# Block 0 of a two-layer kernel: V of the first two tiles from raw x, mended afterwards with weight column sums and norm rows

## The chip, the cores and the metric

The kernel runs on one core of a Trainium2 chip. A core has five engines that run side by side: TensorE (PE, matmuls), VectorE (DVE), ScalarE (ACT), GpSimd (POOL) and SyncE (SP, which here only issues DMAs). The metric is the device time of one execution in microseconds (us); less is better. The time before is 1616.42 us, the median of three runs (1616.15 to 1616.79).

## The reference

The input is one sequence of 2048 tokens with 1024 channels, in bfloat16. Two kinds of layer follow each other twice:

```python
x = x + _A_ref(_layernorm(x), wqkv, wo)                  # attention
x = x + _B_ref(_layernorm(x), W_gate, W_up, W_down)      # gated feed-forward
x = x + _A_ref(_layernorm(x), wqkv, wo)
x = x + _B_ref(_layernorm(x), W_gate, W_up, W_down)
```

`_A_ref` projects the normalized x to Q, K and V, with 32 heads of 32 channels. Each token attends to eight earlier tokens, at distances 0, 2, ..., 14; the softmax runs over these eight, and the result is projected by `wo`. `_B_ref` computes a gate and an up projection of width 3584, multiplies the up projection by the gate's positive part, and projects down. Layer normalization subtracts the mean over the 1024 channels and multiplies by 1/sqrt(variance + 1e-5); call that factor rstd.

## The kernel before

**Tiles and blocks.** The tokens are cut into 16 tiles of 128 (`P`), four tiles (`TPB`) to a block of 512 (`BLK`). All x stays in SBUF, one tile per 128 tokens, in bf16. A projection needs the normalized x with channels on the partitions (`xnT`); it is turned either by PE (a transpose into PSUM and a copy out of it) or by a DMA transpose on SP (`turn`, L282). The 1024 channels are eight chunks of 128 (`kc`), so one output tile of 128 channels by 512 tokens (a "c step") is eight matmuls of 512 columns.

**Weights.** They come in slabs of 1 MB on SP's DMA queue into a ring of five (`wring`); the load of a slab waits on SP until the slab five before it has been read for the last time. The two slabs of V for block 0 are special (`load_slab`, L226): each is loaded in four slices of one chunk, so that the first matmul need not wait for a whole slab. Slabs `v0,0` and `v0,1` hold the chunks 0 to 3 and 4 to 7. Q's two halves, K's two halves and later slabs follow on the same queue, with the x tiles of the next blocks between them.

**Order of the work.** PE instructions are chained in the order in which the program emits them (`pe_group`), those of DVE in the first pass by `dv`, and the DMAs on SP by `sp_dma`; each queue runs strictly in order. The emission order comes from a list of events with planned times (L957 to L1129): `t_v0`, `t_qk0` and so on are starting times of the stages, `GRP` (1.73) is the planned time of one c step. The planned times only sort the events.

**Stages of the first pass.** V of block 0 (`v_first`, L482), Q and K of block 0 (L1014), Q and K of block 1 (staged to DRAM), V of blocks 1 and 2, then within them the head sums of block 0 (`head_mm`, L640) for the softmax of block 0, V of block 3, Q and part of K of blocks 2 and 3, the output projection of block 0 (`wo_steps`, L808), the rest of K, and then the gate and up projections of block 0. DVE meanwhile forms the products of Q with shifted K for block 0 (`prod_sum_steps`, L654), whose sum is the tile `s`; PE adds the heads of `s` (tile `L`); DVE and ACT make the softmax; DVE multiplies by V (`pv_steps`), starts the Q-K products of block 1, and adds the output projection to x (`add`, L828). These additions stand on DVE behind the first products of block 1. The accumulators of all projections share one PSUM ring of six (`psum`, L81), a second area of two banks (`psum_l`) holds `L` and some transposes.

**V of block 0 (L512 to L557).** Nine scratch matmuls run while x is loaded (L442). Tile 0 is centred first: DVE and ACT each sum half of the channels and DVE subtracts the mean (`centre`). PE transposes the centred tile, ACT copies it to `xnT`, and matmuls on single chunks of tile 0 begin. Tile 1 is centred with the batch-norm statistics of DVE (`bn`, `aggr`), turned in two halves between matmuls of tile 0, and joined. The rstd of both tiles is applied afterwards: POOL computes it, splits it into three bf16 parts (`thirds`), PE spreads it over the partitions (`spread_rstd`, tile `rb`), and DVE multiplies V with it on the way out of PSUM (`scaled`) and later `xnT` for Q and K (`widen`). Tiles 2 and 3 are normalized in full before they are turned; their turns and copies (`later`) stand between matmuls of other tiles.

The emission order around the head sums of block 0 is

```python
    spread(v_steps(2, ln_a[2], "v123", True), t_v2, GRP)
    ev.append((t_v2 + 5.2 * GRP, lambda: head_mm(0)))
    spread(softmax_steps(0), t_v2 + 5.3 * GRP, 0.01)
```

so the head sums stand behind the sixth c step of V of block 2.

Of the kernel before, what the change touches and what calls it, by code (L numbers as in the profile page):

```python
# [7 lines left out]
BF16 = mybir.dt.bfloat16  # L8
# [28 lines left out]
def kernel(  # L37
# [123 lines left out]
    k_d = dram.tile([KC, P, S], BF16, name="k_d")  # L161
    s_d = [dram.tile([P, TPB, W, P], BF16, name=f"s_d{i}") for i in range(2)]
# [8 lines left out]
    def load_x(b, tiles=range(TPB)):  # L171
        for t in (b * TPB + i for i in tiles):
            if t == 0:
                sp_dma(x_tiles[t][:, 0:SLAB], x_dram[t * P:(t + 1) * P, 0:SLAB])
                nc.scalar.dma_start(x_tiles[t][:, SLAB:D], x_dram[t * P:(t + 1) * P, SLAB:D])
            elif t == 1:
                nc.scalar.dma_start(x_tiles[t][:], x_dram[t * P:(t + 1) * P, :])
            else:
                sp_dma(x_tiles[t][:], x_dram[t * P:(t + 1) * P, :])
# [42 lines left out]
    def load_slab(key, src):  # L222
# [3 lines left out]
        if key[0] == "v0":  # L226
            for i, (k0, k1) in enumerate(((0, 1), (1, 2), (2, 3), (3, 4)) if key[1] == 0 else ((0, 1), (1, 2), (2, 3), (3, 4))):
                if (key[1], i) == (1, 2):
                    load_x(0, [2, 3])
                sp_dma(tv[:, k0:k1, :], src[:, k0:k1, :])  # L230
# [76 lines left out]
    load_slab(("qk01", "q", 0), qkv_half(0, 0))  # L307
# [10 lines left out]
    def ln_first():  # L318
        hold = {"xnT": xnT_pool.tile([P, TPB, KC, P], BF16, tag="xnT", name="xnT_first")}
        xna = big_tile([P, TPB, D], "xn_first", True)  # L320
        last = {}
# [20 lines left out]
        def aggr(t):  # L342
# [3 lines left out]
            power(t, mv[:, 1:2], 1.0)  # L346

        pair = stat_pool.tile([P, 2], F32, tag="rpair", name="rpair", bufs=1)

        def power(t, var, sign):  # L350
            vpe = small("vpe1")
            rstd[t] = pair[:, t:t + 1] if t < 2 else small("rstd1")[:]
            on("g", nc.gpsimd.tensor_scalar, vpe[:], var, sign, EPS, op0=ALU.mult, op1=ALU.add)
            on("g", nc.gpsimd.tensor_tensor, rstd[t], vpe[:], neg_half[:, 0:1], op=ALU.pow)

        def centre():
            parts = [small("part0"), small("part1")]
            on("v", nc.vector.tensor_scalar, xna[:, 0, 0:SLAB], x_tiles[0][:, 0:SLAB], 1.0 / D, None, op0=ALU.mult,
               op1=ALU.add, accum_out=parts[0][:])
            on("a", nc.scalar.activation, xna[:, 0, SLAB:D], x_tiles[0][:, SLAB:D], ACT.Identity, scale=1.0 / D,  # L360
               accum_out=parts[1][:])
            for h in range(2):
                cols = slice(h * SLAB, (h + 1) * SLAB)
                on("v", nc.vector.tensor_scalar, xna[:, 0, cols], x_tiles[0][:, cols], parts[0][:], parts[1][:],
                   op0=ALU.subtract, op1=ALU.subtract)

        def centre_second():
            for h in range(2):
                cols = slice(h * SLAB, (h + 1) * SLAB)
                on("v", nc.vector.tensor_scalar, xna[:, 1, cols], x_tiles[1][:, cols], mean[1], None, op0=ALU.subtract)  # L370

        def square_of(src):
            sq = small("sq1")
            on("a", nc.scalar.activation, xna[:, 3, :], src, ACT.Square, scale=float(D) ** -0.5, accum_out=sq[:])
            return sq

        def act_mean(t):
            mn = small("mean1")
            on("a", nc.scalar.activation, xna[:, t, :], x_tiles[t][:], ACT.Identity, scale=1.0 / D, accum_out=mn[:])
            mean[t] = mn[:]  # L380

        def act_power(t, sq):
            nvar = small("nvar1")
# [778 lines left out]
```

## Time and profile before

| | |
|---|---|
| median of three runs | 1616.42 us |
| span of the profiled execution, first to last instruction | 1614.4 us |
| median over that span (what lies around it) | 2.0 us |
| PE busy | 1607.8 us (100%) |
| DVE busy | 1141.5 us (71%) |
| ACT busy | 474.9 us (29%) |
| DMA moved | 317.94 MB, mean 197 GB/s |
| granted PE clock, mean | 1.000 |
| Q of block 0 starts on PE | 22.00 us |
| output projection of block 0 starts on PE | 157.33 us |

The page does not give a time of its own for the profiled execution beside its span; the three runs agree within 0.64 us. The profile is a record of one execution. "Busy" of PE counts pipelined matmuls, so it says that PE always has one in flight and not that each goes at its best pace. The chain of waits is followed back from the last instruction: each piece is what the next one had to wait for. In a timeline, the columns are start and duration in us, engine, line, operation, output and inputs, and in brackets the idle time of that engine just before and what ended it.

### The profile page before, as it was taken

The numbers are of one execution on the slowest core, as the hardware profiler recorded it, in microseconds if no ns is written. First come the engines' busy times: TensorE is split into PE (matmuls) and PEld (weight loads), VectorE is DVE, ScalarE is ACT, GpSimd is POOL, SyncE is SP. The second block draws the span as 40 slices with busy tenths as digits, with TensorE's granted clock in tenths as the row PEclk, the third lists the DMA queues.
The fourth block names the chain that finished last, engine by engine and source line by source line (L and its number), as shares of the span: only waits on it lengthen the run. The fifth ranks groups of instructions, "written<-read, shape, count | busy, mean of one in ns | idle before, by whom it ended". The sixth has DMA issues, their size and how long they took to land.

```text
span 1614.4 us, 19048 instructions
## 1 busy us (share of the span) xinstructions
PE 1607.8 (100%) x7657; PEld 790.4 (49%) x7707; DVE 1141.5 (71%) x966; ACT 474.9 (29%) x968; POOL 178.1 (11%) x173
## 2 busy tenths in 40 slices
PE   9999999999999999999999999999999999999999
PEld 7646544444444445444454444544445444444445
DVE  6999979997989698929389393993939939311211
ACT  5753312131115313603136031361313311131110
POOL 2400000010003002300053000530005100000000
PEclk9999999999999999999999999999999999999999
DMA  9767867596668666784747857488574874655452
GB/s 305 186 195 243 215 180 237 184 229 199 201 199 222 197 188 201 201 244 146 227 157 204 235 157 232 151 200 254 165 226 157 205 240 157 210 157 181 157 167 68
DMA packets 359561, 317.94 MB, mean 197 GB/s; under 512 B 105136, under 2 KB 333616, under 8 KB 358960
## 3 DMA queue, kind: packets, MB, share of 16 engines
q1 hardware_dynamic: 358896, 316.13, 66.8%
q8 instruction: 60, 0.98, 0.3%
q10 hardware_dynamic: 576, 0.59, 0.1%
q14 instruction: 29, 0.24, 0.1%
HBM read 266.29 MB, written 34.66 MB: 186 GB/s over the span
## 4 chain that ended last, share of the span: by engine, by line
PE 99%; issue 0%; DVE 0%; DVEq 0%
PE acc_u L132 24%; PE acc_g L132 24%; PE dacc L132 18%; PE acc_v L132 7%; PE acc_k L132 7%; PE acc_q L132 7%; PE acc_wo L132 7%; PE dacc_pair L132 5%; PE scratch L132 0%; DVE x L915 0%; PE tp_pair L432 0%; PE tp L432 0%; PE L L132 0%; PE bc L132 0%; PE tp_second L432 0%
## 5 line engine op out<-in xcount | busy, mean ns | idle before, releaser
L132 PE MATMUL acc_u<-xnT_b,w_u 128*128 128x512 bf16 x1792 | 423.3, 379 | 0.0
L132 PE MATMUL acc_g<-xnT_b,w_g 128*128 128x512 bf16 x1792 | 423.3, 379 | 0.0
L858 ACT ACTIVATE r<-acc_g 128x512 bf16<-128x512 f32 x224 | 133.5, 596 | 724.8 <-PE acc_g L132 687.7
L106 DVE TENSOR_TENSOR hT<-acc_u,r 128x512 bf16<-128x512 f32 x224 | 150.8, 686 | 240.9 <-PE acc_u L132 238.1
L132 PE MATMUL dacc<-w_d,hT 128*128 128x512 bf16 (+2 forms) x1427 | 303.5, 369 | 1.5
L132 PEld LDWEIGHTS <-hT 128*128 128x128 bf16 x1876 | 181.3, 98 | 206.0
L132 PEld LDWEIGHTS <-w_g 128*128 128x128 bf16 x1792 | 175.4, 98 | 211.3
L132 PEld LDWEIGHTS <-w_u 128*128 128x128 bf16 x1792 | 175.3, 98 | 211.5
L106 DVE TENSOR_TENSOR pv<-a,vhm 128x4096 bf16<-128x4096 bf16 x64 | 143.5, 2283 | 0.0
L915 DVE TENSOR_TENSOR x<-dacc,x 128x512 bf16<-128x512 f32 (+2 forms) x40 | 24.9, 654 | 154.2 <-PE dacc L132 154.2
L671 DVE TENSOR_TENSOR t<-q,k 128x2048 f32<-128x2048 bf16 x56 | 128.0, 2292 | 6.7 <-ACT k L606 4.6
L106 DVE TENSOR_TENSOR t<-q,k 128x2048 f32<-128x2048 bf16 x56 | 127.4, 2285 | 3.1 <-ACT k L606 1.6
L106 DVE TENSOR_TENSOR pv<-pv 128x1024 bf16<-128x1024 bf16 (+1 forms) x128 | 113.7, 949 | 0.0
L132 PE MATMUL acc_wo<-w_o,oT 128*128 128x512 bf16 x498 | 111.1, 379 | 0.7
L687 DVE TENSOR_TENSOR ac<-ac,t 128x2048 f32<-128x2048 f32 x48 | 109.7, 2285 | 0.3
L106 DVE TENSOR_TENSOR ac<-ac,t 128x2048 f32<-128x2048 f32 x48 | 109.6, 2283 | 0.0
L612 POOL COPY kh<-k 128x14 bf16<-128x14 bf16 x40 | 51.7, 1296 | 502.3 <-ACT k L606 502.3
L265 POOL TENSOR_TENSOR st_b<-st_b,neg_half 128x1 f32<-128x1 f32 x29 | 43.6, 1511 | 528.5 <-ACT st_b L264 528.5
L132 PE MATMUL dacc_pair<-w_d,hT 128*128 128x512 bf16 (+1 forms) x413 | 92.5, 372 | 0.4
L132 PEld LDWEIGHTS <-oT 128*128 128x128 bf16 x512 | 50.1, 98 | 60.4
L260 ACT ACTIVATE xn_b<-x 128x1024 bf16<-128x1024 bf16 x29 | 30.3, 1045 | 131.3 <-DVE x L106 69.2
L477 ACT CAST vT<-acc_v 128x512 bf16<-128x512 f32 x56 | 32.5, 587 | 57.6 <-PE acc_v L132 56.7
(151 smaller groups left out, 1236.0 us busy)
## 6 DMA issues: line engine op xcount, KB each, us to landing
w_g<-in_B_W_gate_dram SPq DMA_DIRECT2D x56, 1024.0 KB, 7.2
w_u<-in_B_W_up_dram SPq DMA_DIRECT2D x56, 1024.0 KB, 5.5
w_d<-in_B_W_down_dram SPq DMA_DIRECT2D x48, 1024.0 KB, 6.1
w_o<-in_A_wo_dram SPq DMA_DIRECT2D x16, 1024.0 KB, 8.1
vhm<-v_d SPq DMA_DIRECT2D x32, 284.0 KB, 6.8
v_d<-vT SPq DMA_DIRECT2D x8, 1024.0 KB, 9.5
oT<-o_d SPq DMA_DIRECT2D x32, 256.0 KB, 3.8
w_d<-in_B_W_down_dram SPq DMA_DIRECT2D x16, 512.0 KB, 3.7
```

The source lines that it names most:

```text
L106: tail_dve[0] = f(*args, **kwargs).ins
L132: tail_pe[0] = nc.tensor.matmul(*args, **kwargs).ins
L260: nc.scalar.activation(xn, xt[:], ACT.Square, accum_out=sq)
L265: nc.gpsimd.tensor_tensor(rstd, vpe, neg_half[:, 0:1], op=ALU.pow)
L477: tail_act[0] = nc.scalar.copy(st["vT"][:, c, :], acc[:]).ins
L612: nc.gpsimd.tensor_copy(khalo[n][:, c, :], k[:, BLK:BLK + HALO])
L671: nc.vector.tensor_tensor(t[:], i0, i1, op=ALU.mult)
L687: nc.vector.tensor_tensor(o, i0, i1, op=ALU.add)
L858: tail_act[0] = nc.scalar.activation(rs[j][:], acc[:], ACT.Relu).ins
L915: run = dv if n < NB - 2 else (lambda f, *args, **kwargs: f(*args, **kwargs))
```

## The change

V of tiles 0 and 1 is now computed from raw x. Normalization is linear: V of a token is rstd times (raw V minus mean times the column sum of the weights). The matmuls of tile 1 get one more column of ones (tile `xr`), which yields the weights' column sums. ACT keeps the raw products and these sums in f32 (`keep`). The means (negated) and rstd of both tiles are written to DRAM in four rows on ACT's queue (`put_rows`) and read back on SP, spread over all partitions (`get_rows`); DVE then mends V (`mend`). For Q and K, tiles 0 and 1 are normalized in full and turned by DMA transposes on SP (`turn_dma`). `centre`, `centre_second`, the three parts of rstd, `spread_rstd`, `scaled` and `widen` go. Tile 1 is loaded in two halves, as tile 0 was; x tiles 2 and 3 move in the queue; Q's first slab is no longer loaded ahead of the head but behind it. Scratch matmuls go from nine to five. The matmuls of tiles 0 and 1 on chunks 6 and 7 are now ordered by output; tile 2 is then done completely, and tile 3 after it. The statistics of block 1 move later in DVE's order, and the head sums and softmax of block 0 move two c steps later.

The diff, cut to its core:

```diff
+    st_d = dram.tile([4, P], F32, name="st_d")
...
-            if t == 0:
+            if t < 2:
                 sp_dma(x_tiles[t][:, 0:SLAB], x_dram[t * P:(t + 1) * P, 0:SLAB])
                 nc.scalar.dma_start(x_tiles[t][:, SLAB:D], x_dram[t * P:(t + 1) * P, SLAB:D])
-            elif t == 1:
-                nc.scalar.dma_start(x_tiles[t][:], x_dram[t * P:(t + 1) * P, :])
             else:
                 sp_dma(x_tiles[t][:], x_dram[t * P:(t + 1) * P, :])
...
-            for i, (k0, k1) in enumerate(((0, 1), (1, 2), (2, 3), (3, 4)) if key[1] == 0 else ((0, 1), (1, 2), (2, 3), (3, 4))):
-                if (key[1], i) == (1, 2):
-                    load_x(0, [2, 3])
-                sp_dma(tv[:, k0:k1, :], src[:, k0:k1, :])
+            for k in range(KC // 2):
+                if (key[1], k) in ((1, 0), (1, 3)):
+                    load_x(0, [2 if k == 0 else 3])
+                sp_dma(tv[:, k:k + 1, :], src[:, k:k + 1, :])
...
-    load_slab(("qk01", "q", 0), qkv_half(0, 0))
...
+        xr = work.tile([P, KC, 2 * P + 2], BF16, tag="t", name="xr_first")
+        nc.gpsimd.memset(xr[:, :, 2 * P:2 * P + 2], 1.0)
+        st4 = stat_pool.tile([P, 4], F32, tag="st4", name="st4", bufs=1)
...
+            rstd[t] = st4[:, 2 + t:3 + t] if t < 2 else small("rstd1")[:]
+            on("g", nc.gpsimd.tensor_scalar, vpe[:], mv[:, 1:2], 1.0, EPS, op0=ALU.mult, op1=ALU.add)
             on("g", nc.gpsimd.tensor_tensor, rstd[t], vpe[:], neg_half[:, 0:1], op=ALU.pow)
...
+            if t < 2:
+                on("g", nc.gpsimd.tensor_scalar, st4[:, t:t + 1], mv[:, 0:1], -1.0, 0.0, op0=ALU.mult, op1=ALU.add)
+
+        def apply(t):
+            on("v", nc.vector.tensor_scalar, xna[:, t, :], x_tiles[t][:], mean[t], rstd[t],
                op0=ALU.subtract, op1=ALU.mult)
 
+        def put_rows():
+            on("a", nc.scalar.dma_start, st_d[:].rearrange("a p -> p a"), st4[:])
+
+        def get_rows():
+            hold["rows"] = pool["early"].tile([P, 4, P], F32, tag="rows", name="rows", bufs=1)
+            sp_dma(hold["rows"][:], bass.AP(tensor=st_d.tensor, offset=st_d.offset, ap=[[0, P], [P, 4], [1, P]]))
+
+        def turn_dma(t):
+            sp_dma(hold["xnT"][:, t, :, :], xna[:, t, :], True)
...
+            src = x_tiles[t][:] if t < 2 else xna[:, t, :]
...
                 with pe_group():
                     tail_pe[0] = nc.tensor.transpose(tps[t][c // (KC // 2)][:, c % (KC // 2), :],
-                                                     xna[:, t, c * P:(c + 1) * P], ident[:]).ins
-
-        def copy(t, eng, h, i0=0, i1=KC // 2):
+                                                     src[:, c * P:(c + 1) * P], ident[:]).ins
...
+            k = slice(h * (KC // 2), (h + 1) * (KC // 2))
+            on(eng, f, xr[:, k, t * P:(t + 1) * P] if t < 2 else hold["xnT"][:, t, k, :], tps[t][h])
...
-            scratch(9)
-            centre()
-            turn(0)
-            copy(0, "a", 0, 0, KC // 4)
-            copy(0, "a", 0, KC // 4, KC // 2)
...
-            bn(1, 0)
-            bn(1, 1)
-            aggr(1)
-            centre_second()
-            power(0, square_of(xna[:, 0, :])[:], 1.0)
-            hold["thirds"] = thirds()
...
+            scratch(5)
+            for t in range(2):
+                turn(t)
+                copy(t, "v", 0)
+                copy(t, "a", 1)
+            for t in range(2):
+                bn(t, 0)
+                bn(t, 1)
+                aggr(t)
+            put_rows()
...
+        banks, pairs, opened = {}, {}, set()
+        PER = (4, 3)
...
+        def raw_prod(kc, c, t):
+            key, bank = spot(t, c)
+            with pe_group():
+                mm(bank[:, c % PER[t], :], lhsT=slab["v0", kc // (KC // 2)][:, kc % (KC // 2), c * P:(c + 1) * P],
+                   rhs=ln["xr"][:, kc, t * P:(t + 1) * P + t], start=key not in opened, stop=(kc == KC - 1),
+                   skip_group_check=True)
+            opened.add(key)
+
+        def keep(t, i):
+            n = min(PER[t], KC - PER[t] * i)
+            cs = slice(PER[t] * i, PER[t] * i + n)
+            bank = banks[t, i]
+            ln["on"]("a", nc.scalar.copy, st["raw"][:, cs, t * P:(t + 1) * P], bank[:, 0:n, 0:P])
+            if t == 1:
+                ln["on"]("a", nc.scalar.copy, st["cols"][:, cs], bank[:, 0:n, P])
...
+        def mend(i):
+            for c in (2 * i, 2 * i + 1):
+                dv(nc.vector.scalar_tensor_tensor, st["raw"][:, c, :], ln["rows"][:, 0:2, :].rearrange("p a t -> p (a t)"),
+                   st["cols"][:, c:c + 1], st["raw"][:, c, :], op0=ALU.mult, op1=ALU.add)
+            dv(nc.vector.tensor_tensor, st["vT"][:, 2 * i:2 * i + 2, 0:2 * P], st["raw"][:, 2 * i:2 * i + 2, :],
+               _ap(ln["rows"], 2 * P, [[0, 2], [1, 2 * P]]), op=ALU.mult)
...
             st["vT"] = big_tile([P, KC, BLK], "vT_0", True)
+            st["raw"] = work.tile([P, KC, 2 * P], F32, tag="t", name="raw_first")
+            st["cols"] = stat_pool.tile([P, KC], F32, tag="cols", name="cols", bufs=1)
             ln["open_up"]()
...
-            for kc in range(3):
-                chunk(kc, 0)
-            ln["turn"](1, (0,))
-            ln["copy"](1, "v", 0)
...
-            ln["turn"](1, (1,))
-            ln["copy"](1, "a", 1)
-            for kc in range(4):
-                chunk(kc, 1)
-            chunk(4, 0)
-            chunk(4, 1)
...
+            for kc in range(KC - 2):
+                for t in range(2):
+                    for c in range(KC):
+                        raw_prod(kc, c, t)
             ln["bn"](2, 0)
             ln["bn"](2, 1)
             ln["aggr"](2)
-            ln["spread_rstd"]()
+            for t in range(2):
+                ln["apply"](t)
+                ln["turn_dma"](t)
+            ln["get_rows"]()
             ln["apply"](2)
...
+            ln["bn"](3, 0)
+            for t, i in ((0, 0), (1, 0), (0, 1), (None, 0), (1, 1), (1, 2)):
+                if t is None:
+                    ln["turn"](2)
+                    ln["copy"](2, "v", 0)
+                    ln["copy"](2, "v", 1)
+                    continue
+                for c in range(PER[t] * i, min(PER[t] * (i + 1), KC)):
+                    for kc in range(KC - 2, KC):
+                        raw_prod(kc, c, t)
+                keep(t, i)
+            ln["bn"](3, 1)
+            ln["aggr"](3)
+            ln["apply"](3)
+            for c in range(KC):
+                for kc in range(KC):
+                    prod(kc, c, 2)
+            ln["turn"](3)
+            ln["copy"](3, "a", 0)
+            ln["copy"](3, "v", 1)
             for i in range(KC // 2):
-                if i == 2:
-                    later(2)
-                halves(i, 0, 6)
-                if i == 2:
-                    ln["apply"](3)
-                scaled(i)
-            for t in (2, 3):
...
-                        later(3)
-                        ln["widen"]()
-                    for kc in range(KC // 2):
...
-            for i in range(KC // 2):
-                halves(i, 1, KC // 2)
-                ln["on"]("a", nc.scalar.copy, st["vT"][:, 2 * i:2 * i + 2, 2 * P:BLK], pairs[1, i][:])
+                mend(i)
+            for c in range(KC):
+                for kc in range(KC):
+                    prod(kc, c, 3)
+                if c % 2 == 1:
+                    ln["on"]("a", nc.scalar.copy, st["vT"][:, c - 1:c + 1, 2 * P:BLK], pairs[c // 2][:])
...
-    ev.append((0.25, head))
-    ev.append((0.35, lambda: load_x(1, [0, 1])))
+    ev.append((0.15, head))
+    ev.append((0.35, lambda: load_x(1, [0])))
+    ev.append((0.45, lambda: load_x(1, [1])))
     ev.append((t_v0 + GRP * 6 + 0.5, lambda: load_x(1, [2, 3])))
     ev.append((t_v0 + GRP * 6 + 0.6, lambda: load_x(2)))
     ev.append((t_v0 + GRP * 6 + 0.7, zero_v))
     stats, apply, turn, ln_a[1] = ln_steps(1, "a", True, range(TPB))
     for t in range(TPB):
-        ev.append((t_v0 + 7.5 + 2.0 * t, stats[t]))
-        ev.append((t_v0 + 9.6 + 2.0 * t, apply[t]))
-        ev.append((t_v0 + 11.6 + 2.0 * t, turn(t)))
+        ev.append((t_v0 + 11.4 + 2.0 * t, stats[t]))
+        ev.append((t_v0 + 13.5 + 2.0 * t, apply[t]))
+        ev.append((t_v0 + 15.5 + 2.0 * t, turn(t)))
...
-    ev.append((t_v2 + 5.2 * GRP, lambda: head_mm(0)))
-    spread(softmax_steps(0), t_v2 + 5.3 * GRP, 0.01)
+    ev.append((t_v2 + 7.2 * GRP, lambda: head_mm(0)))
+    spread(softmax_steps(0), t_v2 + 7.3 * GRP, 0.01)
```

## The prediction

> **What bounds the kernel now.** I read the page first, then the chain that ended last, then the timeline where the change touches it.
>
> ```profile
> PE 1607.8 (100%) x7657; PEld 790.4 (49%) x7707; DVE 1141.5 (71%) x966; ACT 474.9 (29%) x968; POOL 178.1 (11%) x173
> ```
>
> TensorE (PE) is busy for the whole span of 1614.4 us. A change can therefore move the time only by adding or removing PE work, or by making PE wait. The chain in the first 40 us shows the stage that is rewritten:
>
> ```profile
> 1.13 4.02 PE scratch L132 x9
> 5.15 0.85 PE tp L432 x8
> 6.00 0.03 issue
> 6.03 1.62 PE acc_v L132 x24
> 7.65 0.22 PE tp_pair L432 x4
> 7.87 0.45 PE acc_v L132 x8
> ...
> 22.16 5.18 PE acc_q L132 x24
> ```
>
> Eight transposes take 0.85 us at first (107 ns each) and four take 0.22 us later (55 ns each): PE doubles its pace at about 6.3 us, some 5.2 us after its first matmul. From then on a 128-column matmul costs 56 ns (8 in 0.45). From the first transpose to Q there is almost no gap. Farther on, two places in the DVE timeline and in that of all engines matter:
>
> ```profile
> 98.89 2.29 DVE L106 TENSOR_TENSOR s<-ac,t 128x2048 bf16<-128x2048 f32 x1
> 102.19 0.27 DVE L106 TENSOR_TENSOR L<-L,maskc 32x112 f32<-32x112 f32 x1 [1.00 <-PE L L132]
> ...
> 106.10 1.91 DVE L106 TENSOR_REDUCE ssum<-d 128x128 f32<-128x1024 f32 x1 [1.12 <-ACT d L732]
> ```
>
> ```profile
> 157.33 13.98 PE L132 MATMUL acc_wo<-w_o,oT 128*128 128x512 bf16 x62
> ...
> 164.69 2.29 DVE L106 TENSOR_TENSOR ac<-ac,t 128x2048 f32<-128x2048 f32 x1
> ...
> 166.89 2.48 DVE L106 TENSOR_TENSOR x<-acc_wo,x 128x512 bf16<-128x512 f32 x4
> ```
>
> DVE waits 1.00 us for the head sums (L) at 102.19. From there to the additions at 166.89 the DVE timeline names only one other idle time, 1.12 us for the exponential. PE's output projection and DVE's additions then stand very close to each other (below).
>
> **The front, step by step** (timeline base, where Q starts at 22.00).
>
> *Start.* Nine scratch matmuls start 0.427 us apart (the first transpose starts at 4.94); five end at 3.26. The halves of x tile 0 land at 0.81 + 2.6 = 3.4 and 0.80 + 2.8 = 3.6. Transposes now read raw x, so they start at 3.45, not at 4.94. Sixteen at 107 ns end at 5.16. Tile 1 comes in two halves of 128 KB; whole, it landed at 1.25 + 3.8 = 5.05. Halves land between 3.6 and that; I take 4.1, in time for the second eight.
>
> *Raw matmuls.* The first needs the first weight slice (1.26 + 3.6 = 4.86) and DVE's copy of the turned tile (row: 0.42): 5.25. Ten run at 107 ns until 6.3, the other 86 of the first six slices at 56 ns: done at 11.1. The 129th column for the weight sums adds 64 columns in all, 0.03 us.
>
> *Last slice.* Now each output takes slices 6 and 7 together, so its second matmul needs slice 7. The bytes ahead of that slice are the same as before, and its landing is in the view of the weight tile for 5 to 9 us:
>
> ```profile
> L121 SPq DMA_DIRECT2D w_v<-in_A_wqkv_dram x2: 430/430/430, 5.5 to 6.0; - x2
> ...
> DMA to landing us min/median/max: 5.5/5.6/5.7
> ```
>
> Issued at 5.96, landed at about 11.7. PE goes on at 11.75: the lead of 1.5 us is mostly spent waiting for this DMA.
>
> *Tile 2.* 22 matmuls (1.23), 8 transposes (0.45), 10 matmuls (0.56): 13.99. DVE has tile 2 normalized by about 12.1: copies until 5.8, three times 1.29 + 0.21 of statistics with gaps to 10.4, three applies of 0.55. So PE does not wait for that. Both copies are on DVE, 0.42 each, after the last transpose: 14.05 and 14.5. The first four matmuls wait 0.06, the fifth waits to 14.5; 60 x 0.056 brings 17.85.
>
> *Tile 3.* It is turned with nothing else left to do beside it: 0.45, then ACT's copy (0.59), and after that DVE's (0.42), which in the program waits for ACT's: 19.1 and 19.55. Then 60 x 0.056: Q starts at 22.9 against 22.00, **+0.9**. Before, the copies of tiles 2 and 3 lay beside matmuls of other tiles.
>
> *What SP does later.* Q's weights were issued at 7.00; now they stand on SP behind two DMA transposes, which wait for the applies (about 11.0 and 11.6), and the read-back of the rows. A transpose of one tile occupies SP for 1.25 to 4.04 us in this trace; I take 1.25, since by 11.7 nothing is queued ahead of it. The write of the four rows on ACT's queue has no row: the nearest, 28 KB in small pieces, landed after 2.6 us, the zero halo of the same size after 6.9. I take 2.6, so it lands at 12.7 and hides behind the transposes. Weights then flow from about 15.0. Before, the second half of Q landed 6.5 us after the last V slice (18.2 against 11.7): now 21.5, needed at 23.8. Covered by 2.3 us.
>
> *K's second half.*
>
> ```profile
> SPq L121 <- PE acc_v L132: 8.3, 1, 8.3
> ```
>
> SP held K's second half (issued at 18.7, landed 6.1 later, 24.8) until the first V slab came free. Now tile 3's last output still reads that slab: issue at about 22.7. By the flow it lands at 15.0 + (24.8 - 11.7) = 28.1, by 22.7 + 6.1 at 28.8; needed 6.04 us after Q begins (27.18 + 0.86 - 22.00), at 28.95. I charge **0.1**.
>
> *Mending* has no row: eight 128x256 f32 operations between 0.22 (128x1) and 0.64 (128x512); I take 0.36, with four multiplications of 0.64: 5.4 us of DVE from 19.6 to 25. Block 1's statistics then wait for x tiles 6 and 7, queued behind K's second half (about 29.5). The first Q-K product moves from 30.69 to about 34.5; the idle 1.36 us before the product at 36.91 and others take up part: "s" is some 2 us late.
>
> **The middle.** The head sums stand two V steps later on PE: 16 matmuls x 0.2158 (112 take 24.17 in the chain) = 3.45 us. That hides the late "s" (2 us against 3.45 + 0.41 of slack; at 3.9 PE itself would stop there). But DVE waits for L, so its whole chain moves by 3.45 against PE: the additions at 166.89 move to 170.34. Who waits for them? The output projection has eight accumulators in a ring of six; the seventh waits for the first addition (a DVE wait in the program's order). PE reaches the seventh at 157.33 + 48 x 0.2158 = 167.69; the addition ended at 166.89 + 0.68 = 167.57. The slack is 0.1 us, so PE stalls for **3.35 us**. The second half of W_o on SP stands behind the same DVE work (150.7 + 8.3 = 159.0, now 162.5, needed at 160.8); that stall of 1.7 lies inside the 3.35. Afterwards PE and DVE stand as before, so nothing is paid twice. Bounds: 0 if DVE catches up somewhere the views don't show, 3.45 at most.
>
> **Sum**: 1614.4 + 0.9 + 0.1 + 3.35 = 1618.75 of span. The median of the runs lies 2.0 over the span of the profiled execution (1616.42); so **1620.8**. About 0.2% (3.2 us) is what a measurement of this kernel can tell from no change; 1619.65 is that bound.
>
> **Rivals.**
> *A, a later doubling of the pace.* Before, scratch matmuls filled the time up to the transposes; now sixteen transposes stand between 3.45 and 5.16. If they do not help to raise the clock, the 5.2 us begin at 5.25: 48 matmuls at 107 ns up to 10.4, 48 at 56 ns to 13.1, so 1.35 later than slice 7: 1622.1. For it: the trace never shows the rise without 3.8 us of scratch ahead. Against: it came right behind eight transposes. [...] I give 17%.
> *B, not slower: DVE's delay never reaches PE.* The place is the seventh accumulator. If the chain from L to the additions can give back 3.35 us (a product that today waits unseen for a load), only the front counts: 1617.4, and down to 1616 if slice 7 lands by 11.1. It decides from the point where DVE gets 3.3 of 64 us back. Against it: the pieces follow each other without idle time. 15%.
> *C, SP.* If the two transposes take SP 4.04 and 2.25 us, as they did behind a backlog, weights come 3.8 us later; Q's waits 1.5, K's about 4: 1620.8 + 2.5 to 4, say 1623.8. Against: the queue is nearly empty at 11.7. 8%.
> The forecast keeps 60%.
>
> **How the numbers follow.** The range takes in A, the larger part of B, and ends short of C's middle: 1617.2 to 1623.2. Slower by over 0.2%: nine tenths of the forecast, all of A and C, about 0.78. Within 0.2%: the rest of the forecast and most of B, 0.19. Faster: the low end of B with the front better than worked out, 0.03.
>
> **What would show it.** PE idle some 3.3 us around the output projection at 158 to 172, with the release by a DVE addition; DVE idle about 2 to 3 us before its mask addition near 106; Q beginning near 22.9 with gaps ahead of slice 7 (near 11) and of tile 3's matmuls (near 18.5); K's first outputs without a gap. No gap at the seventh accumulator would make the prediction wrong; a gap before K would mean C.

## The result and the profile after

The changed kernel takes **1627.45 us** (median of five runs, 1626.57 to 1629.89) against 1616.42: a ratio of 1.0072 (95% interval 1.0059 to 1.0084), 11.0 us slower. The forecast was 4.4 us slower (1620.8), with 1623.2 as the upper end of its range. The profiled execution took 1627.23 us, its span is 1625.5.

First the page's line of busy times of the changed kernel, then its view of PE's waits (us in total, times, the longest one):

```profile
PE 1609.8 (99%) x7695; PEld 791.9 (49%) x7745; DVE 1145.0 (70%) x976; ACT 470.9 (29%) x963; POOL 180.8 (11%) x171
```

```profile
PE acc_q L132 <- DMA w_qk_q<-in_A_wqkv_dram: 2.7, 2, 1.6
PE acc_wo L132 <- DVE x L106: 2.1, 1, 2.1
PE acc_k L132 <- DMA w_qk_k<-in_A_wqkv_dram: 1.4, 1, 1.4
```

PE's busy time rose by only 2.0 us; the rest of the 11 us is waiting, in two places. The waits of `acc_wo` (2.1, and 1.0 for its weights) are the stall at the output projection that was forecast. The waits for Q's and K's weights were not. The timeline of PE shows both places:

```profile
6.42 8.62 PE L132 MATMUL raw<-xr_first,w_v 128*128 128x128 bf16 x118 [0.86 <-DMA w_v<-in_A_wqkv_dram]
...
20.96 3.97 PE L132 MATMUL acc_v<-xnT_first,w_v 128*128 128x128 bf16 x64 [0.67 <-ACT xnT_first L329]
26.01 1.08 PE L132 MATMUL acc_q<-xnT_first,w_qk_q 128*128 128x512 bf16 x4 [1.08 <-DMA w_qk_q<-in_A_wqkv_dram]
28.72 4.54 PE L132 MATMUL acc_q<-xnT_first,w_qk_q 128*128 128x512 bf16 x20 [1.63 <-DMA w_qk_q<-in_A_wqkv_dram]
...
35.50 1.09 PE L132 MATMUL acc_k<-xnT_first,w_qk_k 128*128 128x512 bf16 x4 [1.38 <-DMA w_qk_k<-in_A_wqkv_dram]
36.42 1.89 PE L132 MATMUL acc_q<-xnT_first,w_qk_q 128*128 128x512 bf16 x8
...
169.43 7.08 PE L132 MATMUL acc_wo<-w_o,oT 128*128 128x512 bf16 x32 [0.96 <-DMA w_o<-in_A_wo_dram]
178.61 3.61 PE L132 MATMUL acc_wo<-w_o,oT 128*128 128x512 bf16 x15 [2.11 <-DVE x L106]
182.06 4.26 PE L132 MATMUL acc_k<-xnT_a,w_qk_k 128*128 128x512 bf16 x19
```

Two points locate the loss. Their lines in the kernel before:

```profile
28.91 1.89 PE L132 MATMUL acc_q<-xnT_first,w_qk_q 128*128 128x512 bf16 x8
...
171.14 17.43 PE L132 MATMUL acc_k<-xnT_a,w_qk_k 128*128 128x512 bf16 x80
```

The Q step after the first K step starts at 36.42; before, at 28.91: the front costs **7.5 us** (forecast 1.0). The K steps after the output projection start at 182.06; before, at 171.14: 10.9, so the middle costs **3.4 us** (forecast 3.35). Nothing else of that size follows.

In the front, PE ended V some 2.8 us late (24.93; before, 22.17) and then waited for weights for 4.1 us, together 6.9 of the 7.5. Why the weights were late is seen in the DMA traffic. The same windows of the kernel before, and then of the changed one (the last two columns are the DMA engines' busy share and the GB/s moved):

```profile
10.00:13.00 3.00, 3.00 (x51) 2.93 (x49) 2.38 (x7) 2.30 (x4) 0.76 (x3) 1.00 1.02 382
13.00:16.00 3.00, 3.00 (x48) 2.89 (x46) 3.00 (x7) 1.07 (x2) 0.80 (x3) 1.00 1.05 391
16.00:18.00 2.00, 2.00 (x39) 2.00 (x37) 2.00 (x2) 1.07 (x2) 0.00 (x0) 1.00 1.06 388
18.00:20.00 2.00, 2.00 (x26) 1.85 (x24) 1.32 (x3) 0.42 (x1) 0.00 (x0) 1.00 1.07 389
```

```profile
10.00:13.00 3.00, 3.00 (x54) 3.00 (x52) 2.52 (x6) 0.00 (x0) 1.11 (x2) 1.00 1.68 221
13.00:16.00 3.00, 3.00 (x56) 2.93 (x53) 0.48 (x2) 1.66 (x5) 0.00 (x0) 1.00 0.36 27
16.00:18.00 2.00, 2.00 (x35) 1.93 (x34) 1.08 (x3) 0.74 (x4) 0.71 (x3) 1.00 1.19 168
18.00:20.00 2.00, 2.00 (x39) 2.00 (x37) 0.55 (x1) 0.00 (x0) 0.09 (x2) 1.00 0.59 18
```

Before, weights flowed at nearly 390 GB/s in all four windows. Now the DMA engines move almost nothing from 13 to 16 us and again from 18 to 20. Two small transfers lie there; the view of the tile `st_d`, the four rows in DRAM:

```profile
L329 ACTq DMA_DIRECT2D st_d<-st x1: 389/389/389, 10.0 to 10.0; - x1
L121 SPq DMA_DIRECT2D rows<-st_d x1: 347/347/347, 17.4 to 17.4; - x1
...
DMA to landing us min/median/max: 5.2/6.3/7.4
```

The write of 2 KB, issued at 10.0, took 7.4 us to land; the read-back on SP could be issued only then, and Q's weights stand behind it (17.8). Single packets in these windows are far out of line: 256-byte packets of the transposes up to 3031 ns (median 18), and sixteen of the 2 KB packets that start between 18.80 and 19.30, behind the issue of the read-back, 919 to 1267 ns (most packets of that size took 84 ns).

### The profile page after: what moved, and what is told of

The parts are those of the page before. It is cut to its first block, busy times and chain, and to the rows that moved or that the text cites. A ratio compares the mean times of both kernels' runs of the same rounds, so it can differ in the third digit from the quotient of the medians.

```text
span 1625.5 us, 19131 instructions
## 1 busy us (share of the span) xinstructions
PE 1609.8 (99%) x7695; PEld 791.9 (49%) x7745; DVE 1145.0 (70%) x976; ACT 470.9 (29%) x963; POOL 180.8 (11%) x171
## 4 chain that ended last, share of the span: by engine, by line
PE 94%; DVE 4%; DMA 1%; issue 1%; ACT 0%; SPq 0%; DVEq 0%
PE acc_u L132 24%; PE acc_g L132 24%; PE dacc L132 18%; PE acc_wo L132 6%; PE acc_k L132 6%; PE acc_v L132 6%; PE dacc_pair L132 5%; PE acc_q L132 5%; DVE pv L106 2%; DVE ac L106 1%; DMA w_qk_k<-in_A_wqkv_dram 1%; PE raw L132 1%; DVE t L106 0%; DMA w_v<-in_A_wqkv_dram 0%; DVE ohm L106 0%
```

## The experiments

Three suspects stood for the front: the read-back (all 128 partitions read the same 2 KB), the two DMA transposes ahead of the weights, and the write of the rows. The theory at first was the read-back; then the transposes; both fell. Measured beside these runs, the kernel before had medians of 1616.46, 1616.39, 1616.24 and 1616.17.

### The middle: the head sums moved back, and moved alone

```diff
-    ev.append((t_v2 + 7.2 * GRP, lambda: head_mm(0)))
+    ev.append((t_v2 + 5.2 * GRP, lambda: head_mm(0)))
```

(with the softmax beside it) in the changed kernel:

> The changed kernel, with the head sums and the softmax of block 0 back behind the sixth V step. Theory of the middle: DVE waits 3.58 us for these sums in the changed kernel, and the seventh accumulator of the output projection pays 3.4 us for it; s is ready at 109.6 and PE would be there at 109.1, so PE waits 0.5 us and the rest comes back: 1627.4 goes to about 1624.4. Rival (DVE is late in any case, by the mending and the later statistics): no gain, 1627 to 1628, and PE waits some 3 us at the head sums instead.

Measured: 1624.56 (1623.94 to 1625.71), so 2.9 less than the changed kernel; both `acc_wo` waits are gone. The opposite edit in the kernel before:

> The kernel before with only the head sums and the softmax of block 0 moved two V steps later on PE, and nothing else of the change. By the theory of the middle PE stalls at the seventh accumulator of the output projection by 3.45 less the slack of 0.1: 1616.4 + 3.3 = 1619.7. Rival: DVE takes the delay up when the front is not late, 1616.4 to 1617. (Taking this move back out of the changed kernel gave 2.9.)

Measured: 1619.85 (1619.38 to 1624.03), ratio 1.0028 (1.0018 to 1.0037), 3.7 more. In five of its nine executions the mean granted clock is 1.000; their median is 1619.50, so 3.3 more, just as expected. The `acc_wo` lines of its PE timeline:

```profile
162.29 7.08 PE L132 MATMUL acc_wo<-w_o,oT 128*128 128x512 bf16 x32 [0.97 <-DMA w_o<-in_A_wo_dram]
171.47 4.87 PE L132 MATMUL acc_wo<-w_o,oT 128*128 128x512 bf16 x14 [2.10 <-DVE x L106]
```

These are the two waits of the changed kernel, to 0.01 us, without any change in the front. So the two places are independent, and the middle is 2.9 to 3.7 by the medians. (After its wait this execution ran 14 matmuls in 4.87 us, at a granted clock of 0.50; see the last section.)

### The read-back

The rows are filled by POOL and not read:

```diff
-            sp_dma(hold["rows"][:], bass.AP(tensor=st_d.tensor, ...))
+            on("g", nc.gpsimd.memset, hold["rows"][:], 1.0)
```

> The changed kernel without the read-back: the rows tile is filled with ones by POOL, so V of tiles 0 and 1 is not mended rightly; the rows are still written. Theory of the read-back: it holds SP until 17.43 and then the DMA engines until 22.6; without it Q's weights are issued at 15.6, land at about 20.5 and 23, and neither Q nor K waits for them: Q begins at 24.9, 4 us come back, 1623.3. Rival (the two DMA transposes hold the queue): Q's second half still lands after 26, under 1.5 us come back, 1626 or more.

Measured: 1626.46 (1624.83 to 1627.22). Only 1.0 us came back, and the ranges overlap; as the sole cause the read-back fell. Two more kernels, also without the read-back, put a read of 256 KB of x into its place, whose data nothing uses: once from 128 different rows, once the same 2 KB row for all partitions.

```diff
+            sp_dma(idle[:], x_dram[0:P, :])                                                   # 128 rows
+            sp_dma(idle[:], bass.AP(tensor=x_dram.tensor, offset=..., ap=[[0, P], [1, D]]))   # one row
```

> As the run without read-back (rows filled with ones, V of two tiles not mended rightly), but at the place of the read-back SP loads the same 256 KB from 128 different DRAM rows of x into a tile that nobody reads, waiting for no write. By the theory that it is the one 2 KB source that is slow: 0.7 us of DMA at the usual 84 ns per 2 KB packet, hidden, 1623.5. By the rival that any 256 KB at this place costs it: 1625 or more.

> As the run before, but all 128 partitions read the same 2 KB row of x, which nobody has written in this execution, and without waiting for a write. By the theory of the one source: packets of over 1000 ns as in the changed kernel, the engines held for some 3 us, Q's second half at about 26.5 and K's at 33: half of the 4 us is lost again, about 1625.5. By the rival that only rows just written are slow to read: as with 128 rows, 1623.5, packets of 84 ns.

Measured: 1626.19 (1625.59 to 1627.75) with 128 rows, 1629.74 (1629.09 to 1630.37) with one, some 4 us above its expectation. The bytes cost nothing here (1626.19 against 1626.46 without a read), the single source 3.5 us (1629.74 against 1626.19). Not all of that is the read: in the profiled executions Q's second half lets PE go on 2.4 us later (29.50 against 27.09), and with one source the granted clock then fell to 0.50 from 27.35 to 34.18 and again from 180.95 to 184.37, with 128 rows never. One window of each, first with 128 rows, then with one:

```profile
20.00:22.00 2.00, 1.43 (x23) 1.31 (x23) 1.49 (x4) 0.62 (x2) 0.00 (x0) 1.00 1.05 374
```

```profile
20.00:22.00 2.00, 1.25 (x20) 1.02 (x18) 1.21 (x3) 0.58 (x1) 0.00 (x0) 1.00 0.98 130
```

With one source the DMA engines are busy (0.98) and move a third (130 against 374 GB/s). So the read is slow, as suspected, but taking it out shows that something else holds the queue as well.

### The write or the transposes

From the kernel without the read-back, once the write is left out too and the transposes stay, once the transposes are left out and the write stays:

```diff
-            put_rows()
```

```diff
-            sp_dma(hold["xnT"][:, t, :, :], xna[:, t, :], True)
+            on("g", nc.gpsimd.memset, hold["xnT"][:, t, :, :], 1.0)
```

> The changed kernel with neither the write of the four rows nor their read-back (the rows are filled with ones, so V of tiles 0 and 1 is not mended rightly); the two DMA transposes stay. The write's completion came only 7.4 us after its issue in the changed kernel and 9.2 us in the one without the read, so it is a suspect for the jam. Theory T (the two transposes themselves hold the queue): 1626.4 as without the read alone, the transposes land at about 17 to 20 us and Q still waits some 2 us for its weights. [...]

> The changed kernel with the write of the rows, but without their read-back (rows filled with ones) and without the two DMA transposes (the normalized x of tiles 0 and 1 for Q and K is filled with ones, so Q, K and V of these tiles are wrong). Theory T: Q's weights are issued near 12 and land by 18 and 21, the waits for Q's and K's first weights go (2.0 and 1.4 us in the kernel without the read), what stays is V's later end, about 2.5 us, and the 3.4 us of the middle: 1616.4 + 2.5 + 3.4 = 1622.3 to 1623. Rival W (the write jams the queue): 1626, as without the read alone. Rival R (K's second half, released only when V's first slab is free, sets the time of K's start whatever the transposes do): Q does not wait but K does, 1624.5.

Measured: **1622.63** (1622.38 to 1623.45) without the write, 1625.60 (1624.60 to 1626.96) without the transposes. Rival W holds, theory T falls: without the write the transposes land 3.9 to 4.2 us after issue, Q waits for nothing and K for 0.44 us:

```profile
24.35 5.35 PE L132 MATMUL acc_q<-xnT_first,w_qk_q 128*128 128x512 bf16 x24
...
31.00 1.09 PE L132 MATMUL acc_k<-xnT_first,w_qk_k 128*128 128x512 bf16 x4 [0.44 <-DMA w_qk_k<-in_A_wqkv_dram]
```

The profile of the changed kernel counts the 4-byte packets of the write on q10 and those of the transposes and weights on q1; how the one holds up the other isn't shown. With the write and without any transpose, the weights themselves get stuck:

```profile
13.00:16.00 3.00, 3.00 (x54) 2.86 (x52) 1.89 (x5) 2.17 (x8) 1.31 (x4) 1.00 1.13 358
16.00:18.00 2.00, 2.00 (x40) 2.00 (x38) 0.55 (x1) 0.00 (x0) 0.57 (x2) 1.00 1.02 110
18.00:20.00 2.00, 1.25 (x20) 1.01 (x18) 0.58 (x2) 0.59 (x1) 0.00 (x0) 1.00 1.13 114
20.00:22.00 2.00, 2.00 (x38) 2.00 (x37) 1.97 (x5) 0.93 (x2) 0.00 (x0) 1.00 0.77 115
22.00:24.00 2.00, 2.00 (x30) 1.68 (x27) 1.93 (x5) 1.39 (x3) 0.00 (x0) 1.00 0.42 80
```

For eight microseconds the engines move 80 to 115 GB/s where they moved 358, and this write, issued at 9.8, lands 12.6 us later.

### Order and clock

Q's two slabs ahead of the transposes:

```diff
     load_slab(("v0", 1), qkv_half(2, 1))
+    load_slab(("qk01", "q", 0), qkv_half(0, 0))
+    load_slab(("qk01", "q", 1), qkv_half(0, 1))
```

> The changed kernel in full, with both halves of Q's weights (2 MB) issued on SP directly behind V's last slice, ahead of the two transposes. Theory T: Q's weights land by about 19, no wait for them (2.7 us in the changed kernel); the transposes move behind them and land at 21 to 23, in time for Q at 24.9, so 1624.7, if K's weights come no later than now. Rival (the transposes are slow whatever stands around them, 6 us or more from issue, and now start behind 2 MB): they land after 25, Q waits for them instead, K's weights come later still, and the time stays at 1627 or goes up.

Measured: 1627.88 (1625.92 to 1628.06). The rival's outcome: the transposes now land 10.8 and 13.2 us after issue, Q waits for them (1.4 us) and K for its weights (2.6). What is stuck only changes its name. Two scratch matmuls in PE's pause ahead of the first slice:

```diff
             ln["open_up"]()
+            bank = spot(0, 0)[1]
+            for _ in range(2):
+                with pe_group():
+                    mm(bank[:], lhsT=ones[:], rhs=_ap(ones, 0, [[0, 4], [1, P]]), start=True, stop=True, ...)
```

> The changed kernel with two more scratch matmuls between the transposes of raw x and the first raw product, in place of the pause of PE before the first weight slice. Theory of the clock: the pace doubles some 5 us after PE's first matmul if PE isn't left idle meanwhile, so it now doubles at about 6.5 instead of 10.25, the raw products of the first six slices end by 12, and V ends 1 to 1.5 us earlier (23.5 to 24); since Q's weights land at 26 to 28.7 all the same, the total stays within 0.5 us of the changed kernel, 1627.2. [...] Another way to go: V's earlier end brings K's second half forward by as much, and 1 us of the total.

Measured: 1628.08 (1625.87 to 1628.75), no gain, as expected. PE's timeline, with V's end at 23.20 (24.64 less the wait of 1.44) in place of 24.93 and a longer wait for Q's weights behind it:

```profile
5.92 5.65 PE L132 MATMUL raw<-xr_first,w_v 128*128 128x128 bf16 x97
11.95 1.36 PE L132 MATMUL raw<-xr_first,w_v 128*128 128x128 bf16 x21 [0.38 <-DMA w_v<-in_A_wqkv_dram]
...
24.64 1.09 PE L132 MATMUL acc_q<-xnT_first,w_qk_q 128*128 128x512 bf16 x4 [1.44 <-DMA w_qk_q<-in_A_wqkv_dram]
```

The pace was the fast one at once. But this run doesn't show that the pause is what delays it: its trace records the clock's rise at 5.19, where the added matmuls only start. And of the eleven kernels with the changed front and without these two matmuls (the changed one included), six ran their raw products fast from about the start too, and five only from 9.6 to 10.3 us on, with the same instructions up to there. (The clock column of the windows doesn't tell them apart: the traces hold no clock record ahead of the rise, and the column shows 1.00 there.)

### What about the write is slow

From the kernel without the read-back (1626.46; without the write 1622.63), the same 2 KB written in another layout: 128 pieces of 16 bytes side by side, or 512 pieces of 4 bytes, each 512 bytes from the next.

```diff
-    st_d = dram.tile([4, P], F32, name="st_d")
+    st_d = dram.tile([P, 4], F32, name="st_d")       # 16-byte pieces, written from st4 as it is
+    st_d = dram.tile([4, P, P], F32, name="st_d")    # 4-byte pieces apart, written to st_d[:, :, 0]
```

> The changed kernel without the read-back (rows filled with ones; V of tiles 0 and 1 is not mended rightly), and the same 2 KB of rows written in another layout: 128 pieces of 16 bytes, side by side in DRAM, in place of 512 pieces of 4 bytes. With the 4-byte write this kernel took 1626.46, without any write 1622.63. Theory S (the cost is per small piece): a quarter of the pieces jams a quarter as long, about 1623.6. Theory L (the cost comes from many engines writing into the same 2 KB of DRAM at once, whatever the pieces): it jams about as before, 1625 to 1626.5.

> As the one before, but again 512 pieces of 4 bytes, each to a place of its own 512 bytes from the next, so 256 KB of DRAM are touched in place of 2 KB. Theory S (per small piece): 1626.5, packets of the weights held up from about 15 to 18 us, the transposes land after 18. Theory L (the same place in DRAM): no jam, the transposes land by 16.5, no wait for Q's weights, 1622.6 as without any write.

Measured: 1623.96 (1622.11 to 1624.60) and **1622.50** (1622.17 to 1623.68). The number and size of the pieces are the same in the second, and the whole jam is gone: theory S falls. The first kernel alone would have fitted S.

To see whether the write needs anything else of the change, it was added to the kernel before, from a constant tile, with nothing waiting for it:

```diff
             hold["thirds"] = thirds()
+            on("a", nc.scalar.dma_start, st_d[:].rearrange("a p -> p a"), neg_half[:])
```

> The kernel before with one added DMA that nothing waits for: 512 pieces of 4 bytes into one 2 KB tensor on ACT's queue, issued after ACT's square at about 10 us, as the changed kernel does. If the write alone jams the queue, weights packets in flight from 13 to 24 us flow at a quarter of their rate for some 8 us, so Q's second half (landed 18.2 before, needed at 22.9) and K's second half (24.8, needed at 28) come some 6 us later: waits of 1.5 us for Q and 1 to 2 us for K, 1616.4 + 3 = 1619.4. If the jam needs the changed order (transposes or weights queued behind it), 1616.4.

> The kernel before with the same added write that nothing waits for, 512 pieces of 4 bytes at the same point on ACT's queue, but each piece 512 bytes from the next (256 KB of DRAM touched). With all pieces in one 2 KB tensor the kernel went from 1616.24 to 1622.56. If the shared place is what jams (as in the changed kernel without the read, 1626.46 against 1622.50 apart), the time is that of the kernel before, 1616.4. If the number of small pieces on the queue counts by itself, 1619 or more.

> The kernel before with the same 2 KB written in 128 pieces of 16 bytes side by side, so four pieces share 64 bytes in place of sixteen. If the jam grows with the pieces that meet in one place, a quarter of them holds the queue a quarter as long, some 2 us, which Q's slack of 4.7 us covers: 1616.4 to 1617. If any write of 128 partitions into one 2 KB jams alike, 1622.

Measured: 4-byte pieces side by side **1622.56** (1621.59 to 1624.18, ratio 1.0040, 1.0025 to 1.0055); apart 1616.30 (ratio 1.0002, 0.9992 to 1.0011); 16-byte pieces side by side 1616.28 (1.0002, 0.9993 to 1.0011). A 2 KB write that nothing reads costs 6.3 us, by its addresses alone. Its own time to land isn't the cost: apart, it took 8.5 us to land and held up nothing. Windows of the first, then two of them of the second:

```profile
13.00:16.00 3.00, 3.00 (x48) 2.89 (x46) 3.00 (x7) 1.10 (x3) 0.80 (x3) 1.00 1.19 163
16.00:18.00 2.00, 2.00 (x39) 2.00 (x37) 2.00 (x3) 1.05 (x2) 0.00 (x0) 1.00 0.96 82
18.00:20.00 2.00, 2.00 (x27) 1.84 (x24) 0.33 (x1) 0.47 (x1) 0.00 (x0) 1.00 0.73 40
20.00:22.00 2.00, 2.00 (x21) 1.81 (x19) 0.00 (x0) 1.28 (x3) 0.00 (x0) 1.00 0.36 39
```

```profile
16.00:18.00 2.00, 2.00 (x40) 2.00 (x38) 2.00 (x3) 0.86 (x3) 0.00 (x0) 1.00 1.05 399
18.00:20.00 2.00, 2.00 (x37) 1.98 (x35) 1.35 (x2) 0.31 (x1) 0.00 (x0) 1.00 1.05 402
```

My expectation for the first, 3 us, was half of what it did, and the jam itself is not what it missed:

```profile
25.42 6.23 PE L132 MATMUL acc_q<-xnT_first,w_qk_q 128*128 128x512 bf16 x20 [2.45 <-DMA w_qk_q<-in_A_wqkv_dram]
```

Of the 5.4 us of its profiled execution (1621.59), 2.45 are this wait, the only one for weights; 1.9 are half clock behind it (the granted clock is 0.50 from 26 to 28 us; these 20 matmuls take 6.23 us, where the changed kernel's took 4.54; the eight of K behind them 2.12 for 1.89); some 0.8 comes later, where PE waits 0.6 us for `s` at the head sums. The write was also issued earlier than expected, at 7.5 in place of 10.

### What is left of the change

The changed kernel with the head sums early and the rows in 16-byte pieces (the read-back stays, the mending reads the rows with a step of four):

> The changed kernel with two repairs: the head sums at their old place, and the rows written in 128 pieces of 16 bytes and read back in that order (the mending reads them with a step of four). From 1627.45: the write's jam goes (2.5 by the kernel without the read, 1626.46 to 1623.96), the middle's 2.9 goes: 1622.0. The read from one 2 KB place stays; if it costs as much as the read of one row of x did (3.5 over a read of 128 rows) and nothing hides it any more, 1625.

Measured: 1622.43 (1620.97 to 1622.82), near the first of its two values. Its trace still has waits of 0.57 us for Q's weights and 1.38 for K's; that the read-back causes them isn't shown. And with the rows spread by PE, with no DRAM in between:

```diff
-            sp_dma(hold["rows"][:], bass.AP(tensor=st_d.tensor, ...))
+            for j in range(4):
+                for i, part in enumerate(hold["parts"]):
+                    mm(bc[:, j, :], lhsT=_ap(part, j, [[0, P]]), rhs=ident[:], start=(i == 0), stop=(i == 2))
+            on("v", nc.vector.tensor_copy, hold["rows"][:], bc[:, 0:4, :])
...
+    load_slab(("qk01", "q", 0), qkv_half(0, 0))
...
-            ln["turn"](3)                 # behind tile 2's products; now in the middle of them
```

> The changed kernel mended by what the runs so far point to: the four rows are spread over the partitions by 12 matmuls from three bf16 parts, with no DRAM write or read; Q's first half is issued ahead of the transposes as in the kernel before; the head sums stand at their old place; two scratch matmuls fill PE's pause ahead of the first slice; tile 3 is turned in the middle of tile 2's products; tile 3's products read V's first slab first. Raw products from 5.9, last slice at 12, tile 2 from 14.3 to 18.4 with tile 3's turn, rows 0.7, tile 3 to 22.8, so Q starts 0.8 later than in the kernel before; K's second half is issued some 2 us earlier than in the changed kernel and is in time; some 0.3 from the middle: 1617.5. If the jam has another cause than the write and the read, Q or K still wait: 1620 or more. If the front is better than the old one after all: below 1616.

Measured: 1619.14 (1618.91 to 1619.92, ratio 1.0018, 1.0008 to 1.0027). PE waits for no weight of Q or K any more. The time is 1.6 us over the forecast; the trace, of an execution of 1619.92, shows these waits: x of tile 0 lands late (0.65), the last slice (0.67), tile 3's normalized x (0.62) and, in the middle, 0.7 at the head sums for a late `s`. Q starts at 24.41, still behind the 22.00 of the kernel before. No version here beats that one.

## Why the prediction was wrong, step by step

- **Start.** Transposes of raw x at 3.66 (forecast 3.45): right.
- **First slice: wrong.** "The first needs the first weight slice (1.26 + 3.6 = 4.86)" took the old row as it was, though the change puts half of tile 1 on SP ahead of that slice: issued at 1.75, it landed 4.62 later, at 6.37. In executions where the pace is fast from the start this hides in the wait for the last slice, as forecast, but that slice came later too: the work on it starts at 11.95 with more scratch and at 12.07 to 13.06 in the six others, against 11.75. The forecast took over the old issue at 5.96; in the changed kernel it is 7.02.
- **The pace.** Rival A happened in the profiled execution: 107 ns up to 10.24, so V ended at 24.93 and not at 22.9. With the early pace it ended at 23.20 in the kernel with more scratch and at 23.25 in the one without transposes by DMA (24.35 in the one without rows, late). The size was about right (1.35 forecast; 1.1 and 1.7 between such pairs); the chance of 17% was too low for five of eleven.
- **Why early or late.** The clock records of the traces tell the two apart. Within each execution all recorded changes lie whole steps of 3.413 us apart (with one row of x as the source the stretches are 17.067, 6.827, 146.773 and 3.413 us: 5, 2, 43 and 1 steps); where the steps fall differs from one execution to the next. In the five early ones with such records the clock rises at 4.98 to 5.71, in the five late ones at 9.60 to 10.29. So the late ones have a step that ends at 6.19 to 6.88 without a rise, and PE's pause behind the transposes (0.50 to 0.87 us) lies wholly or mostly in it; an early rise leaves at most 0.2 us of pause ahead of it. That the pause in such a step puts off the rise is argued from this and not shown: the two kernels that fill the pause had early steps anyway (5.19 and 4.80). Had it gone as in rival A, with transposes that don't help and 5.2 us that begin with the raw products, all eleven should have been late; six were not, and in the five with records the rise comes 0.2 to 1.6 us ahead of the first raw product. Whether the transposes count towards it beside the scratch matmuls, no run here separates.
- **SP: this is the step that failed.** "The write of the four rows on ACT's queue has no row: the nearest, 28 KB in small pieces, landed after 2.6 us [...]. I take 2.6, so it lands at 12.7 and hides behind the transposes. Weights then flow from about 15.0." The write landed at 17.4, the weights were issued at 17.8, Q's second half landed at 28.7 (forecast 21.5) and K's at 35.45 (28.8). Of two rows, 2.6 and 6.9, I took the lower, and 7.4 was measured; but above all I charged the write only its own latency, and what it does to the transfers beside it was no term of the sum. The runs price it at 3.8 us in this kernel (1626.46 to 1622.63; 2.95 between the two timelines, 34.88 to 31.93, neither of which has a fall of the clock) and at 6.3 us in the kernel before, half clock included.
- **The read-back** was counted as one more DMA on SP; taking it out gave 1.0 us, behind the write's jam.
- **Rival C** named the right place (Q and K wait for weights, 1623.8) with the wrong mechanism. SP did spend 1.37 and 3.05 us on the transposes, but without the write they took 1.35 and 2.04 and Q didn't wait.
- **Mending.** 0.48 and 0.69 us for 0.36 and 0.64; `s` is ready 8.4 us later, not 2. PE itself is 7.5 later by then, so this cost nothing in the changed kernel.
- **The middle.** 3.35 forecast, 0.96 + 2.11 of waits and 3.4 between the two timelines: right in place, releaser and size. Rival B falls.

The sum of what the runs show, by the medians: write 3.8, read-back 1.0, middle 2.9 to 3.7, and the remaining 2.5 to 3.3 for V's later end (24.35 against 22.00 in the kernel without rows) and a K wait of 0.4: 11.0. By the timelines, none of them with a fall of the clock: 3.0 for V's later end and that K wait (31.93 against 28.91), 2.95 for the write, 1.5 for the read-back together with the late pace (36.42 against 34.88), 3.4 for the middle: 10.9. Not shown are what makes the jam, and from which distance on it ends: 4-byte pieces were written side by side and 512 bytes apart, 16-byte pieces side by side, and no other layout was tried.

## What to carry to other kernels

Price a small DMA not by its bytes but by where its pieces meet: 512 words of 4 bytes side by side in 2 KB of DRAM, written from 128 partitions, cost 6.3 us in a kernel with a full weight queue, and nothing there when they lay 512 bytes apart or came as 16-byte pieces (in the changed kernel without the read-back the 16-byte pieces still took 1623.96 against 1622.63 without a write, with ranges that overlap). When weights are late, compare the GB/s of the same windows in two kernels. Here that showed the jams, whether the DMA engines were busy (0.98, 130 against 374 GB/s from 20 to 22 us, with one row as the source and with 128) or not (0.36, 27 against 391 GB/s from 13 to 16 us, in the changed kernel and in the one before). How long a transfer takes to land doesn't name the cause: the write apart took 8.5 us and held up nothing, while the transposes, both times without the read-back, took 7.3 and 7.7 us with the write beside them and 3.9 and 4.2 without it. A move of two steps in one engine's order was worth 3.4 us (forecast 3.35) 60 us later, and could be forecast from the slack of 0.1 us of the one accumulator that bound.

## What the runs showed of the hardware

- All partitions reading one 2 KB row, beside the jam of the write: 2 KB packets of up to 1038 ns (most of those beside the read of 128 rows took 84, the longest 845), 130 against 374 GB/s, and Q's second half 2.4 us later than with a read of 128 rows.
- A PE wait can cost more than its length: the kernel before with late head sums took 1621.20 to 1621.61 in the three executions with a mean granted clock of 0.999, and 1619.50 (median) in the five with 1.000. In some executions a wait of some 2 us was followed by half the granted clock (the column ahead of the last two), always for one or two steps of 3.413 us. Two waits of nearly the same length differ in it by how they fall into the steps. The kernel before with late head sums, whose wait of 2.10 ends at 171.47, step by step, and then the changed kernel, whose wait of 2.11 ends at 178.61:

```profile
168.39:171.80 3.41, 1.31 (x7) 0.53 (x6) 3.41 (x4) 0.00 (x0) 0.00 (x0) 1.00 1.04 146
171.80:175.21 3.41, 3.41 (x10) 1.21 (x8) 2.96 (x7) 2.51 (x6) 0.24 (x1) 0.50 0.00 0
```

```profile
174.06:177.47 3.41, 2.45 (x12) 0.99 (x11) 3.41 (x2) 0.00 (x0) 0.00 (x0) 1.00 1.00 174
177.47:180.88 3.41, 2.21 (x10) 1.07 (x11) 3.41 (x7) 1.09 (x2) 0.00 (x0) 1.00 0.33 37
180.88:184.29 3.41, 3.41 (x18) 2.05 (x16) 2.61 (x7) 2.56 (x9) 1.10 (x2) 1.00 0.76 226
```

In the first the whole wait lies in one step, PE is busy for 1.31 us of it, and the next step runs at 0.50. In the second the end of a step cuts the wait in two, PE is busy for 2.45 and 2.21 us, and the clock stays at 1.00. The other falls fit: the steps ahead of them had PE busy for 0.90 to 1.50 us. The least without a fall are 1.48 (without read-back) and 1.50 (128 rows), so in these traces the border lies at about 1.5 of 3.41 us.
